# A linear-attention and token-mixing kernel on one core: V's parts issued apart, the output weights in three transfers, and a newly searched order of all work

## The chip, the core and the metric

The kernel runs on one NeuronCore of a Trainium2 chip. Five engines work side by side, each through its own list of instructions in order: TensorE (PE; its weight loads are shown as PEld), VectorE (DVE), ScalarE (ACT), GpSimd (POOL) and SyncE (SP), which here only issues transfers. Transfers between the chip's main memory and the on-chip memory are carried out by 16 DMA engines. Matmul results go to PSUM, eight banks of on-chip accumulators, from which VectorE and ScalarE copy them out. The metric is the device time of one launch in microseconds; the profile shows one execution.

## What is computed

Two layers follow each other. The first is a recurrence with decay over 768 time steps, for 4 batches and 8 heads of width 48; the second mixes tokens:

```python
# first layer: y, for every batch and head
cur = u*k_t (outer) v_t
y_t = r_t @ (state + cur)
state = w_t[:, None] * state + k_t (outer) v_t

# second layer on x = y with the heads side by side (4, 768, 384)
wq, wk = x @ w_q, x @ w_k                      # d_hyper = 64
mixed  = (wq @ wk.T) / sqrt(64) @ x            # per batch, 768 x 768 weights
out    = relu(mixed) @ w_out                   # 384 x 384
```

Inputs and output are float32, 4.7 MB for each of r, k, v, w and for the output, 0.8 MB for the weights.

## The kernel before

The time steps are cut into 12 units (n = 0 to 11) of 256 steps, three to a batch; a unit holds two chunks of 128 steps. Each unit needs four tiles of 128 rows x 768 floats (384 KB): `wg`, `kg`, `rg` and `vg`, each from a ring of four buffers, so that the tile of unit n + 4 can be loaded once the tile of unit n has been read. The work of a unit, by the names that stand in the profile:

- `lw` = ln of w (L536, ScalarE); a matmul with the mask `CM` gives its sums along time, and two exponentials of them, `ep` and `en` (L589, L595, ScalarE).
- casts of k, r and v to bf16: `k16`, `r16` (L547; shown as k and r) and `v16` (L687; shown as v), on GpSimd, ScalarE or, for unit 0, VectorE. k and r are transposed on TensorE; `ks` is the copy of k transposed, `qT` = r times ks, `RT` = r times ep (L650), `KT` = k times en (L663, on GpSimd or VectorE; L658 for the first and last unit).
- `VB` is v with its rows sorted (a matmul and a copy); `dd` the diagonal with u, `Vd` = VB times dd (L725).
- `AM` = masked scores of a chunk (L746, VectorE); `kd` (L454 to L462) the keys for the state; `SB` the state (L809); `X` = the first layer's output (L851, VectorE).
- per unit of the second layer: `XT` (X transposed and copied), the products with w_q and w_k, copied to `QK`; per batch `T` and its copy `TS`; per unit again `mx` and its relu `MX` (L466 on ScalarE, L468 on VectorE), the product with w_out, its copy `os`, and the store (L977).

Helpers record most operations, so many groups share a line: L306 is every matmul, L454 and L460 are the plain copies of ScalarE and VectorE.

Nothing is scheduled while the kernel is built. Every operation is a step of the class `Plan`, with an engine or a choice of engines, a duration, and the steps that it waits for. Two tables that were searched beforehand settle the rest: `RANK` gives each step's place on its engine, `ALT` the engine or form for each step that has a choice. `Plan.order` walks through the steps with these tables and a model of durations and of transfers, gives out the PSUM banks and buffers on the way, and emits the instructions in the order in which it placed them. The durations of the model have no effect on the chip but through that order.

Transfers are steps of SyncE. The tile of v of the units 2 to 11 (`SPARE`) is loaded in three transfers that one step issues one right after the other: 64 rows, 63 rows and 1 row (`cuts`). The three weight matrices are one step of three transfers, the output weights (576 KB) in one of them; their three casts (L494 to L496) are one step of GpSimd. Outputs are stored by SyncE, but for the last one, which ScalarE issues. In the model of `order` there is a queue `Q` and a queue `R` of transfers: each transfer takes `dur` on Q and `high` on R, instruction fetches block R for a while, and a transfer starts only when the third one before it has moved.

TensorE also runs 39 matmuls of zeros (`Z`) at the start and in gaps of the first units.

Of the kernel before, what the change touches and what calls it, by code (L numbers as in the profile page):

```python
# [33 lines left out]
class Plan:  # L34
# [8 lines left out]
    ASIDE, BLOCKED = 1200, 1000  # L43
# [45 lines left out]
    def dma(self, key, issue, dur, fn, after=(), buf=None, reads=(), behind=None, high=None):  # L89

        i = self.add(key, {"S": issue}, fn, after, buf, lag=0, behind=behind)
        m = self.add(key + ("wire",), {"Q": (dur, dur if high is None else high, None)}, None, [i], lag=0)
        l = self.add(key + ("land",), {"L": self.LAND}, None, [m], lag=0, reads=reads)
        return i, l

    def order(self):
# [5 lines left out]
        wires = {}  # L102
# [6 lines left out]
        owners, moved, done, mode = [None] * 8, [], [], 0  # L109
# [14 lines left out]
        def start(s):  # L124
# [7 lines left out]
            if s["eng"] == "S" and len(moved) >= 3:  # L132
                t = max(t, moved[-3])
# [30 lines left out]
        while True:  # L164
# [14 lines left out]
            if e == "E":  # L179
                mode = s["mode"]  # L180
            took = s["dur"] + self.SWITCH * change
            n = s["opts"][s["way"]][5]
            if n:
                first = count
                count += n
                while count > edge:
# [5 lines left out]
                    free["R"] = max(free["R"], cross + self.ASIDE) + self.BLOCKED  # L192
                    edge += self.BLOCK
            lock = s["lock"] and e == "D"
            if lock:
                took += max(0, free["P"] - t)
            run(s, t, took)
            if lock:
                free["P"] = max(free["P"], t + took)
            if s["i"] in wires:  # L200
                m = wires[s["i"]]
                free["Q"] = max(free["Q"], s["end"]) + m["dur"]
                free["R"] = max(free["R"], s["end"]) + m["mode"]
                m["start"], m["end"] = s["end"], max(free["Q"], free["R"])
                done.append(m)
                moved.append(m["end"])
# [849 lines left out]
```

## Time and profile before

| | us |
|---|---|
| median of 3 runs | 106.12 |
| range of these | 105.59 to 106.23 |
| profiled execution | 106.6 |
| its span, first to last instruction | 104.8 |
| mean granted TensorE clock | 0.984 of full |

Busy shares overlap, since the engines work side by side. A row of the view by stretch gives for each engine its busy time in that stretch and, in brackets, its instructions; then the granted TensorE clock, the mean share in which the DMA engines were occupied (above 1 where packets overlap) and the rate. A row of a group gives busy time and mean duration (ns) of one instruction, then the idle time of the engine just before it and what ended that. A row of the chain or of the timeline gives start, duration and work. SPq, ACTq and so on are the engines' issuing sides: the duration of an issue includes the time in which it is held up.

### The profile page before, as it was taken

Reading aid. Unit: us, or ns where it says so; the run is one execution under the profiler, and the core shown is the slowest. Engines: PE = TensorE matmul, PEld = TensorE weight load, DVE = VectorE, ACT = ScalarE, POOL = GpSimd, SP = SyncE. Lnnn points to the kernel's source line nnn. Section 1 sums busy time; section 2 is a strip of 40 time slices with the busy share of each in tenths; the row PEclk is TensorE's granted clock in tenths of the full one; section 3 lists DMA queues with packets and bytes.
Section 4 is the critical chain, followed back from the end, with each engine's and each line's share of the span. In section 5 each row is a group of like instructions: output and inputs, shape, how many; then the busy total and the mean of one; then the engine's idle time right before and its main releaser. Section 6 shows DMA issues by size and latency. Waiting matters only on the chain.

```text
span 104.8 us, 5072 instructions
## 1 busy us (share of the span) xinstructions
PE 91.6 (87%) x2201; PEld 65.7 (63%) x2201; DVE 84.3 (80%) x152; ACT 80.0 (76%) x117; POOL 66.9 (64%) x70
## 2 busy tenths in 40 slices
PE   6999998887699789999589689998999999999940
PEld 2264885485567558786375577865777778787510
DVE  5539999898699939999789699998999899857630
ACT  4359879989777298795996988999959898873830
POOL 4433695978998936988589779779995910400000
PEclk9999999999999957999999999999999999999999
DMA  1999997989999999889898999999989100029784
GB/s 33 317 323 325 325 318 183 282 228 244 264 315 267 235 298 248 215 199 280 226 228 199 248 304 307 222 317 301 304 283 326 43 0 6 6 111 367 274 287 172
DMA packets 53488, 24.71 MB, mean 236 GB/s; under 512 B 51162, under 2 KB 52314, under 8 KB 53466
## 3 DMA queue, kind: packets, MB, share of 16 engines
q1 hardware_dynamic: 53306, 24.19, 83.4%
q8 instruction: 17, 0.28, 1.1%
q10 hardware_dynamic: 160, 0.20, 0.5%
q14 instruction: 5, 0.04, 0.1%
HBM read 19.66 MB, written 4.72 MB: 233 GB/s over the span
## 4 chain that ended last, share of the span: by engine, by line
PE 38%; DMA 26%; SPq 9%; ACT 8%; POOL 6%; issue 5%; DVE 4%; POOLq 0%; ACTq 0%; DVEq 0%
PE PS L306 38%; DMA wg<-in_w_dram 13%; DMA vg<-in_v_dram 8%; SPq L364 8%; DMA kg<-in_k_dram 5%; ACT MX L466 3%; DVE AM L746 2%; POOL r L547 2%; POOL k L547 2%; POOL Vd L725 1%; ACT os L454 1%; ACT en L595 1%; SPq L977 1%; DVE VB L460 1%; ACT lw L536 1%
## 5 line engine op out<-in xcount | busy, mean ns | idle before, releaser
L746 DVE TENSOR_TENSOR AM<-PS,US 128x1024 bf16<-128x1024 f32 x24 | 29.0, 1220 | 2.8 <-PE PS L306 2.8
L725 POOL TENSOR_TENSOR Vd<-VB,dd 128x768 bf16<-128x768 bf16 (+1 forms) x13 | 17.6, 1353 | 8.3 <-DVE dd L460 6.1
L663 POOL TENSOR_TENSOR KT<-ks,en 128x1024 bf16<-128x1024 bf16 x10 | 21.3, 2129 | 0.8 <-ACT ep L589 0.7
L595 ACT ACTIVATE en<-PS,dn 128x1024 bf16<-128x1024 f32 (+1 forms) x14 | 13.9, 992 | 2.9 <-PE PS L306 2.4
L306 PE MATMUL PS<-Z 128*128 128x512 bf16 (+1 forms) x43 | 14.8, 432 | 1.1 <-DVE Z L380 1.0
L536 ACT ACTIVATE lw<-wg 128x768 bf16<-128x768 f32 x12 | 10.1, 842 | 6.3 <-DMA wg<-in_w_dram 6.2
L589 ACT ACTIVATE ep<-PS,up 128x1024 bf16<-128x1024 f32 (+1 forms) x14 | 13.9, 1011 | 1.0 <-PE PS L306 0.8
L306 PE MATMUL PS<-wo,MX 128*128 128x384 bf16 (+1 forms) x93 | 13.8, 327 | 0.3 <-ACT MX L466 0.3
L306 PEld LDWEIGHTS <-KT 48*128 48x128 bf16 x352 | 9.1, 95 | 6.9 <-issue 4.0
L547 POOL CAST k<-kg 128x768 bf16<-128x768 f32 x10 | 8.3, 825 | 6.0 <-DMA kg<-in_k_dram 4.7
L851 DVE TENSOR_TENSOR X<-PS,Vd 128x768 bf16<-128x768 f32 (+1 forms) x13 | 11.5, 892 | 0.7 <-PE PS L306 0.4
L306 PE MATMUL PS<-RT,KT 48*128 48x128 bf16 x192 | 9.9, 220 | 1.4 <-ACT QK L454 0.9
L466 ACT ACTIVATE MX<-PS 128x768 bf16<-128x768 f32 (+1 forms) x14 | 9.4, 700 | 1.9 <-PE PS L306 1.9
L687 POOL CAST v<-vg 128x768 bf16<-128x768 f32 x9 | 7.4, 827 | 4.3 <-DMA vg<-in_v_dram 4.1
L547 POOL CAST r<-rg 128x768 bf16<-128x768 f32 x10 | 8.3, 827 | 2.3 <-DMA rg<-in_r_dram 2.3
L650 DVE TENSOR_TENSOR RT<-PS,ep 128x1024 bf16<-128x1024 bf16 (+1 forms) x14 | 8.4, 607 | 1.6 <-PE PS L306 1.4
L454 ACT CAST VB<-PS 128x768 bf16<-128x768 f32 x11 | 8.9, 807 | 1.0 <-issue 0.6
L454 ACT COPY os<-PS 128x768 f32<-128x768 f32 (+1 forms) x10 | 7.0, 702 | 3.3 <-PE PS L306 2.1
L306 PEld LDWEIGHTS <-MX 128*128 128x128 bf16 (+1 forms) x93 | 7.1, 103 | 3.5 <-ACT MX L466 0.4
L306 PE MATMUL PS<-CM,lw 64*128 64x128 bf16 x192 | 8.2, 231 | 1.2 <-ACT lw L536 1.0
L641 DVE TENSOR_TENSOR qT<-PS,ks 128x1024 bf16<-128x1024 bf16 x12 | 8.2, 683 | 0.4 <-PE PS L306 0.3
L809 DVE TENSOR_TENSOR SB<-PS,ep 128x192 bf16<-128x192 f32 x20 | 7.0, 350 | 1.8 <-PE PS L306 1.7
(88 smaller groups left out, 184.9 us busy)
## 6 DMA issues: line engine op xcount, KB each, us to landing
wg<-in_w_dram SPq DMA_DIRECT2D x12, 384.0 KB
kg<-in_k_dram SPq DMA_DIRECT2D x12, 384.0 KB
rg<-in_r_dram SPq DMA_DIRECT2D x12, 384.0 KB
out_dram<-os SPq DMA_DIRECT2D x9, 384.0 KB
vg<-in_v_dram SPq DMA_DIRECT2D x10, 192.0 KB
vg<-in_v_dram SPq DMA_DIRECT2D x10, 189.0 KB
out_dram<-os SPq DMA_DIRECT2D x5, 192.0 KB
vg<-in_v_dram SPq DMA_DIRECT2D x2, 384.0 KB
```

The lines of the kernel that those rows point to most:

```text
L306: return nc.tensor.matmul(o, l, rr, start=start, stop=stop, skip_group_check=True, is_transpose=trans)
L454: nc.scalar.copy(o, i)
L466: nc.scalar.activation(o, i, ACT.Relu)
L536: nc.scalar.activation(view(lw.tile, 0, [[64, H], [512, 2], [1, D]]), view(g["wg"].tile, 0, [[D2, H], [D, 2], [1, D]]), ACT.Ln, bias=0.0, ...
L547: op(view(o.tile, 0, [[64, H], [512, 2], [1, D]]), view(g[src].tile, 0, [[D2, H], [D, 2], [1, D]]))
L589: nc.scalar.activation(view(ep.tile, cs[0] * NP * EW + RS, [[EW, n4], [1 - RS, 2], [1, R]]), view(at(cw), cs[0] * 512, [[C, n4], [R, 2], [ ...
L595: nc.scalar.activation(en.tile[:, ds(cs[0] * 512, w_)], at(cw)[:, ds(cs[0] * 512, w_)], ACT.Exp, bias=dn, scale=-1.0)
L650: nc.vector.tensor_tensor(view(RT.tile, cs[0] * 512, [[512, len(cs)], [R, H], [1, R]]), view(at(kr, BF16), cs[0] * apart + second, [[apart ...
L663: x.tensor_tensor(KT.tile[:, w], ks.tile[:, w], en.tile[:, w], ALU.mult)
L725: (nc.vector if e == "D" else nc.gpsimd).tensor_tensor(Vd.tile[:, cols], VB.tile[:, cols], view(dd.tile, cs[0] * H, [[1, len(cs) * H], [0, ...
L746: AMs[c] = add(("AM", n, c), {"D": 1221}, lambda e, c=c, A=A: nc.vector.tensor_tensor(view(AM[c].tile, 0, [[C, 8], [1, C]]), view(at(A), 0 ...
L851: lambda e, c0=c0, nc_=nc_: nc.vector.tensor_tensor(view(X.tile, (2 * i + c0) * DM, [[D2, NP * nc_], [D, 2], [1, D]]), view(at(y), c0 * NP ...
```

## The change

Every operation stays. Five things change.

1. The model of transfers inside `Plan.order`: no wait for the third transfer before, no fetch blocks on R; instead an issue ends once the work still queued on Q and on R has fallen below a limit each (`DEEP`), and a tile takes 1500 on R (1220 in the first two units). This code is for the search; on the chip it acts through the order alone.
2. V of the units 2 to 11 is three steps instead of one, so that other transfers may stand between its parts: 63 rows, 1 row, 64 rows. The cast `v16` waits for all three.
3. The weights are two steps: w_q and w_k, and the output weights in three transfers of 63, 63 and 2 rows. The casts wait for both.
4. `RANK` and `ALT` are new throughout: the order on all engines and the choice of engines and forms.
5. The class's durations for some DMA steps.

```diff
-    ASIDE, BLOCKED = 1200, 1000
+    DEEP = dict(Q=1850, R=2500)
...
-            if s["eng"] == "S" and len(moved) >= 3:
-                t = max(t, moved[-3])
...
-                    free["R"] = max(free["R"], cross + self.ASIDE) + self.BLOCKED
...
+            if s["i"] in wires:
+                m = wires[s["i"]]
+                x = t + took
+                full = [0]
+                for q, d in (("Q", m["dur"]), ("R", m["mode"])):
+                    if d:
+                        free[q] = max(free[q], x)
+                        full.append(free[q] + m["opts"]["Q"][5] * d // max(m["dur"], 1) - self.DEEP[q])
+                        free[q] += d
+                m["start"] = x
...
+                took = max(took, max(full) - t)
...
-            nc.sync.dma_start(out=view(wo_f, 0, [[DM, NK], [1, DM]]),
-                              in_=moe_w_out.rearrange("(n p) d -> p n d", p=128))
-        l = plan.dma(("wts",), 1800, 2700, f)[1]
+
+        def f_o(e):
+            for p, z in ((0, 63), (63, 126), (126, 128)):
+                nc.sync.dma_start(out=view(wo_f, 0, [[DM, NK], [1, DM]], p0=p, pn=z - p),
+                                  in_=moe_w_out.rearrange("(n p) d -> p n d", p=128)[ds(p, z - p)])
+        l = [plan.dma(("wts",), 1000, 700, f, deep=900, high=850)[1],
+             plan.dma(("wtso",), 1500, 3300, f_o, high=0, deep=800)[1]]
...
-        wts["qk"] = wts["o"] = add(("wcast",), {"P": 2650}, cast, [l])
+        wts["qk"] = wts["o"] = add(("wcast",), {"P": 2650}, cast, l)
...
-            cuts = (0, 64, 127, C) if name == "vg" and n in SPARE else (0, C)
-            g[name + "L"] = plan.dma((name, n), 570 * (len(cuts) - 1) if "S" in begun else 1055,
...
+            t, issue, rest = 1220 if n < 2 else 1500, 500 if "S" in begun else 1055, None
+            if name == "vg" and n in SPARE:
+                g["vl"] = [plan.dma(("vl", n), 500, 1065, lambda e, f=f: f(e, p0=64, p1=127),
+                                    buf=g[name], high=0)[1]]
+                g["vl"].append(plan.dma(("vk", n), 500, 20, lambda e, f=f: f(e, p0=127, p1=C),
+                                        buf=g[name], high=0)[1])
+                g["vgL"] = plan.dma((name, n), 500, 610, lambda e, f=f: f(e, p0=0, p1=64),
+                                    buf=g[name], high=750)
+            else:
+                g[name + "L"] = plan.dma((name, n), issue, 1220, f, buf=g[name], high=t,
+                                         behind=begun.get("S") if n == 0 else None)
...
-                view(g["vg"].tile, 0, [[D2, H], [D, 2], [1, D]])), [g["vgL"]], v16, [g["vg"]])
+                view(g["vg"].tile, 0, [[D2, H], [D, 2], [1, D]])), [g["vgL"]] + g.get("vl", []), v16,
+                [g["vg"]])
```

In the built program this gives the following order of transfers around the middle and the end of the loads (unit in brackets, rows of a part behind the colon):

```
before: ... w8 v8:64 v8:63 v8:1 r8 k8 w9 r9 k9 w10 v9:64 v9:63 v9:1 w11 k10 r10 r11 k11 v10:64 v10:63 v10:1
        store store v11:64 v11:63 v11:1 store ...
after:  ... k8 k9 w8 v8:63 w9 r8 v8:1 v8:64 store v9:63 v9:1 r9 r10 w10 k10 v9:64 store v10:63 w11 v11:63 v11:1
        r11 v10:1 v10:64 k11 v11:64 store ...
```

The engines' work by count: two KT, one wide Vd and two r casts leave GpSimd; VectorE has two KT, one wide Vd, two wide MX and one ks more and three XT, one VB, one wide os and one r less; ScalarE has three r, three XT, one VB and one wide os more and two wide MX, one ks, one wide kd and one v less. TensorE issues 2,220 matmuls instead of 2,201, since some steps use the form with 64 columns of weights at a time where others give it up.

More of the change, by code (lines that the diff above doesn't have):

```diff
@@ L87, in add, with dma @@
         return s
-    def dma(self, key, issue, dur, fn, after=(), buf=None, reads=(), behind=None, high=None):
+    def dma(self, key, issue, dur, fn, after=(), buf=None, reads=(), behind=None, high=None,
+            deep=None):
         i = self.add(key, {"S": issue}, fn, after, buf, lag=0, behind=behind)
         m = self.add(key + ("wire",), {"Q": (dur, dur if high is None else high, None)}, None, [i], lag=0)
+        m["opts"]["Q"][5] = dur if deep is None else deep
         l = self.add(key + ("land",), {"L": self.LAND}, None, [m], lag=0, reads=reads)
@@ L108, in order @@
         rings = {k: [] for k in self.rings}
-        owners, moved, done, mode = [None] * 8, [], [], 0
+        owners, done, mode = [None] * 8, [], 0
         count, edge, ready = 0, self.FIRST, 0
@@ L196, in order @@
                 took += max(0, free["P"] - t)
+            if s["i"] in wires:
[8 more added lines that the diff above has]
+                m["start"] = x
+                m["end"] = max([x] + [free[q] for q, d in (("Q", m["dur"]), ("R", m["mode"])) if d])
+                took = max(took, max(full) - t)
+                for q, d in (("Q", m["dur"]), ("R", m["mode"])):
+                    if d:
+                        free[q] = max(free[q], t + took)
+                        m["end"] = max(m["end"], t + took)
             run(s, t, took)
@@ L360, with load @@
     dn = const([C, 1], F32, "dn")
-    def load(b, i, tl, ap, cuts=(0, C)):
-        for p, z in zip(cuts, cuts[1:]):
-            nc.sync.dma_start(
-                out=view(tl, 0, [[D2, H], [1, D2]], p0=p, pn=z - p),
-                in_=ap[b, :, ds(i * U + 2 * p, 2 * (z - p))].rearrange("h (p j) d -> p h (j d)", j=2))
+    def load(b, i, tl, ap, p, z):
+        nc.sync.dma_start(
+            out=view(tl, 0, [[D2, H], [1, D2]], p0=p, pn=z - p),
+            in_=ap[b, :, ds(i * U + 2 * p, 2 * (z - p))].rearrange("h (p j) d -> p h (j d)", j=2))
     def load_whole(b, q, tl):
```

22 lines of the change are left out of this document (8 added, 14 removed), and 70 rows, old and new, of the table RANK.

## The prediction, made before the result was known

> **What bounds the kernel now.** I read the page first (busy shares, transfer rate, chain of waits), then busy time by stretch, then the chain in order of time, and last the groups of instructions by shape.
>
> ```profile
> PE 91.6 (87%) x2201; PEld 65.7 (63%) x2201; DVE 84.3 (80%) x152; ACT 80.0 (76%) x117; POOL 66.9 (64%) x70
> ...
> PE 38%; DMA 26%; SPq 9%; ACT 8%; POOL 6%; issue 5%; DVE 4%; POOLq 0%; ACTq 0%; DVEq 0%
> ```
>
> No engine is full, and a quarter of the chain is waiting for transfers. The next view cuts the span at the places where the feeding changes, and at 83.58 us, where VectorE starts the first product of the last unit. Columns: PE, PEld, DVE, ACT, POOL busy, granted clock, share of the DMA engines, GB/s.
>
> ```profile
> 5.40:16.00 10.60, 10.57 (x183) 7.18 (x182) 8.65 (x17) 8.16 (x13) 6.45 (x8) 1.00 1.15 318
> 17.00:18.00 1.00, 0.98 (x26) 0.66 (x25) 1.00 (x3) 1.00 (x3) 0.30 (x1) 1.00 0.70 191
> 16.00:36.00 20.00, 17.29 (x476) 12.69 (x475) 17.41 (x27) 15.77 (x21) 17.20 (x16) 1.00 0.97 252
> 36.00:42.00 6.00, 5.03 (x103) 3.56 (x101) 4.28 (x8) 5.31 (x8) 3.56 (x4) 0.72 1.05 276
> 42.00:50.00 8.00, 7.52 (x233) 5.97 (x230) 7.64 (x12) 6.09 (x11) 7.35 (x7) 1.00 0.93 234
> 50.00:60.00 10.00, 7.46 (x200) 5.39 (x196) 8.01 (x12) 9.05 (x13) 7.85 (x7) 1.00 0.89 222
> 60.00:70.00 10.00, 9.71 (x279) 7.61 (x279) 9.63 (x16) 8.87 (x13) 7.82 (x8) 1.00 1.13 286
> 70.00:83.58 13.58, 12.91 (x359) 9.61 (x353) 12.41 (x20) 11.45 (x17) 12.27 (x11) 1.00 0.83 259
> 16.00:83.58 67.58, 59.92 (x1628) 44.83 (x1627) 59.38 (x89) 56.54 (x80) 56.05 (x49) 0.97 0.96 254
> 83.58:104.80 21.22, 16.70 (x386) 12.39 (x382) 13.58 (x27) 13.16 (x24) 1.78 (x2) 1.00 0.41 151
> ```
>
> Up to 16 us the loads run at 318 GB/s. After that the same queue gives 254 on average: 254 x 67.58 is 17.2 MB, which at 318 would take 54 us, so the stream has about 13 us of slack that it spends idle or uneven. At 17 to 18 us, with V in its three parts under way, the rate is 191 at a share of 0.70: 0.6 of 318 and 1.15.
>
> VectorE is the fullest engine of the middle: 59.38 of 67.58 us, 0.879. The shortfall sits in three stretches, 16 to 36, 36 to 42 and 50 to 60: 29.70 of 36 us (0.825). The other three hold 29.68 of 31.58, 0.940, and the best single one 0.963. The chain says what starves the bad ones and what the end hangs on.
>
> ```profile
> 27.62 8.40 DMA wg<-in_w_dram
> ...
> 36.10 0.85 ACT lw L536
> ...
> 76.68 4.35 DMA vg<-in_v_dram
> ...
> 81.95 0.84 POOL k L547
> 82.79 0.05 issue
> 82.83 3.39 PE PS L306 x94
> ```
>
> The w of unit 5 lands 8.40 us after its issue; ScalarE, VectorE and TensorE run dry, and the granted clock falls to 0.72 just there. At the end the last V lands at 81.03, its cast goes first, and the k of the last unit is cast only at 81.95 although it was loaded before: everything of unit 11 starts from that cast.
>
> **The change part by part.** The operations are the same; what moves is the order on every engine, who does which copy, and the order of the transfers.
>
> *Who does what.* By count of the two orders against these groups:
>
> ```profile
> L650 DVE TENSOR_TENSOR RT<-PS,ep 128x1024 bf16<-128x1024 bf16 x10 | 6.8, 684 | 1.6 <-PE PS L306 1.4 <-issue 0.3
> L851 DVE TENSOR_TENSOR X<-PS,Vd 128x768 bf16<-128x768 f32 x11 | 10.5, 953 | 0.4 <-PE PS L306 0.2
> L460 DVE COPY ks<-PS 128x1024 bf16<-128x1024 bf16 x10 | 6.9, 687 | 1.6 <-PE PS L306 1.4
> L460 DVE COPY XT<-PS 128x768 bf16<-128x768 bf16 x6 | 3.3, 551 | 0.1
> L460 DVE COPY os<-PS 128x768 f32<-128x768 f32 x2 | 1.9, 959 | 0.5 <-PE PS L306 0.5
> L462 DVE TENSOR_SCALAR kd<-PS 128x768 bf16<-128x768 bf16 x2 | 1.1, 558 | 0.3 <-PE PS L306 0.3
> L547 DVE CAST r<-rg 128x768 bf16<-128x768 f32 x1 | 0.6, 560 | 0.8 <-DMA rg<-in_r_dram 0.8
> L725 DVE TENSOR_TENSOR Vd<-VB,dd 128x384 bf16<-128x384 bf16 x1 | 0.6, 559 | 0.0
> L468 DVE TENSOR_SCALAR MX<-PS 128x384 bf16<-128x384 f32 x1 | 0.6, 558 | 1.0 <-PE PS L306 1.0
> ...
> L466 ACT ACTIVATE MX<-PS 128x768 bf16<-128x768 f32 x9 | 7.2, 817 | 0.9 <-PE PS L306 0.9
> L454 ACT COPY XT<-PS 128x768 bf16<-128x768 bf16 x5 | 4.0, 794 | 0.2 <-PE PS L306 0.2
> L547 ACT CAST r<-rg 128x768 bf16<-128x768 f32 x1 | 0.8, 846 | 0.0
> L454 ACT COPY ks<-PS 128x1024 bf16<-128x1024 bf16 x2 | 2.0, 1012 | 1.1 <-PE PS L306 1.1
> ...
> L663 POOL TENSOR_TENSOR KT<-ks,en 128x1024 bf16<-128x1024 bf16 x10 | 21.3, 2129 | 0.8 <-ACT ep L589 0.7
> L725 POOL TENSOR_TENSOR Vd<-VB,dd 128x768 bf16<-128x768 bf16 x10 | 14.8, 1478 | 1.6 <-DVE VB L460 1.6
> L547 POOL CAST r<-rg 128x768 bf16<-128x768 f32 x10 | 8.3, 827 | 2.3 <-DMA rg<-in_r_dram 2.3
> ```
>
> VectorE gives up three XT (3 x 0.551), a VB and a wide os (0.959 each; the VB has the os's shape) and an r (0.560): 4.13 us. It takes two KT, one wide Vd, two wide MX, a ks (0.687), a wide kd (0.558) and a narrow os (0.558, by the narrow MX). No row shows a wide KT, Vd or MX on VectorE. KT lies between the 0.684 of RT, a product of the same size, and GpSimd's 2.129; I take 0.684, RT being the same engine. Vd lies between its narrow 0.559 and GpSimd's 1.478; I take X's 0.953. MX I take as the wide os, 0.959. Together 6.04, so VectorE gains 1.9 us of work (with the upper ends 5.3). The narrow copies left over on both sides I let cancel. ScalarE takes three r, three XT, a VB and an os and gives two MX, a ks, a v and a wide kd (taken as an r and an XT): 3 x 0.846 + 5 x 0.794 - 2 x 0.817 - 1.012 - 0.846 - 0.794, 2.2 us more; it gives back five narrow copies for two, so 2.2 is an upper end, and it idles 11 us in the middle (56.54 of 67.58), which covers it. GpSimd sheds two KT, a Vd, two r and takes a v: 4.26 + 1.48 + 0.83, 6.6 us less.
>
> *The last unit.* In the new order an X (0.953) no longer stands on VectorE between the last unit's first products and its masks, where the old one has it, and on TensorE 359 matmuls instead of 418 stand from the last k transposes on. Fifty-nine at 16.70/386 = 43 ns are 2.5 us. So the tail shortens by between 0.95 and 2.5; I take 0.95, since X lies on a chain of products and the matmuls also fill gaps. What leaves the tail has to be done before: VectorE's middle is then 59.38 + 1.9 + 0.95 = 62.2 us of work. On GpSimd the last k is now cast before the last v, so that the v landing no longer holds it; but the last k load itself is now the last but one transfer.
>
> *V in parts.* The 64-row, the 63-row and the 1-row part are now separate steps, placed apart with whole tiles between them. Same bytes, same number of issues. The 0.6 ratio at 17 us is what parts side by side cost; between whole tiles that loss can be covered by them. The price: V is complete only with its last part, one to five transfers later than before from unit 3 on, and a v cast that waits holds GpSimd's queue: behind the casts of units 5 and 6 stand KT of 6 and k of 7. A whole tile is 393 kB, 1.24 us at 318; so 1.2 to 6.2 us if the stream keeps its present pace, nothing if it gains as much of its 13; I take nothing, and the slower case below holds the other end.
>
> *The weights.* One 590 kB transfer becomes 63 + 63 + 2 rows: 1.85 us at 318, 3.1 at 191. The casts of the weights now stand on GpSimd ahead of v of unit 3 and k and r of unit 4. Between 0 and 1.2 us; GpSimd's 2.8 idle us from 16 to 36 hide it and I take 0. Two more issues of SyncE take the 0.49 of the row below each; SyncE's issue of a tile lasts 1.22 us where 0.49 can do, so they pass in its waits.
>
> *Stores and early loads.*
>
> ```profile
> 25.51 0.49 SPq L489 DMA_DIRECT2D wof<-in_moe_w_out_dram  x1
> ...
> 57.67 0.78 ACT L454 COPY os<-PS 128x768 f32<-128x768 f32 x1
> 59.61 1.22 SPq L364 DMA_DIRECT2D kg<-in_k_dram  x1
> ...
> 12.77 0.82 POOL L547 CAST k<-kg 128x768 bf16<-128x768 f32 x1 [0.20 <-DMA kg<-in_k_dram]
> 19.26 2.13 POOL L663 TENSOR_TENSOR KT<-ks,en 128x1024 bf16<-128x1024 bf16 x1
> ```
>
> The first store now has 38 tiles ahead of it and ten behind it, and waits for ScalarE's first os. In the old order SyncE has issued 38 tiles by 59.61 and that copy ends at 58.45; so the store stops no load unless the stream is over 1 us ahead, and even then seven tiles and two stores at 1.24 and three V's at 1.6 (half at 318, half at 191), 16 us in all, bring the last landing to between 75 and, with the 4.35 us that the old last V took from issue to landing, 79 us, against 81.03. Early on, k of unit 2 goes from the 8th to the 12th place among the tiles: it lands four tiles and 0.4 us for the uneven V later, at 18.1 instead of 12.7; r lands a tile after it at 19.4, its cast takes 0.83, and KT, which stands behind that cast, begins at 20.2 instead of 19.26: 0 to 1.0 us, and I take 0.8, nearer the upper end, since KT's place leaves no choice.
>
> *The sum.* With VectorE's middle at the 0.940 that the undisturbed stretches show, 62.2 us of work take 66.2: -1.4. Tail -0.95, unit 2 +0.8. That is -1.5 on a span of 104.8; the profiled execution took 106.6, 1.8 above its span, and the median of the runs is 106.12, so 104.6.
>
> **The rivals.**
>
> *VectorE becomes the bound and the end is later.* The 1.9 us come from an engine with slack (56.05 of 67.58) to the fullest one. If loads still come as late as now, 0.879, then 62.2 takes 70.8, +3.2, less 0.95: 108.4. It decides at 62.2/68.5 = 0.908: below that the kernel is slower. For it: the V's complete later, the late unit 2. Against it: 60 to 70 us ran at 0.963 with the loads at 286 GB/s.
>
> *The stream runs tight.* All at 0.963: 62.2 takes 64.6, -2.9, with the tail 102.3. For it: 13 us of slack in the stream; against it, 70 to 83.58 us is well supplied and still at 0.914.
>
> *The parts move nothing.* The waits change place only and half of the shortfall stays, 0.91: 68.4, +0.8, less 0.95: 106.0. The Trainium skill, DMA: Bandwidth & Descriptors, Rules for kernel authors, says not to cut a transfer in partition halves, since both halves use the same engines one after the other; by that rule the parts gain nothing wherever they stand. The trace agrees only in part: at a share of 0.70 against 1.15 the engines are not all in use.
>
> *VectorE's products wait for GpSimd.* Two KT, a wide and a narrow Vd read two tensors of on-chip memory beside a busy GpSimd. A GpSimd operation lasts 56.05/49 = 1.14 us there; half of it at a share of 0.83 is 0.47, four times 1.9 us, which would make 106.5. The Trainium skill, SBUF — State Buffer, on the shared port pair, says that such a VectorE operation and a GpSimd one that reads that memory exclude each other for a whole instruction. No row of this profile shows the pair.
>
> **How the numbers follow.** The forecast, 104.6 (own range 103.6 to 105.6), gets 0.38; the slower VectorE 0.26; the tight stream 0.14; parts that move nothing 0.11; the products' waits 0.11. About 1% (105.06 and 107.18) is what a measurement of this kernel can tell from no change. Faster: 0.30 of the forecast, the tight stream and a little of the next, 0.45. Slower: 0.24 of the second case and 0.06 of the last two, 0.30. Same: 0.25. The range, 102.5 to 108.3, leaves out half of the tight stream and under half of the slower case.
>
> **What would show it.** In the profile after: VectorE busy 86 us, GpSimd 60; the middle's VectorE share near 0.94 with no clock below 1.00 around 36 us; a rate over 280 GB/s from 16 us on; the cast of the last k ending before 82 us; fewer than 20 us from the last unit's first KT to the end. The forecast is wrong if the middle's share stays under 0.908, if SyncE stands at its first store while loads wait behind it, or if KT on VectorE takes well over 0.684.

## The result and the profile after

| | before | after |
|---|---|---|
| median, us (four runs each, side by side) | 106.18 | 111.97 |
| range, us | 105.59 to 108.35 | 110.92 to 113.66 |
| profiled execution, its span | 106.6, 104.8 | 112.78, 111.1 |

The changed kernel is slower: ratio 1.047, 95% interval 1.041 to 1.053. Runs of one version spread by up to 4 us here, some of them disturbed; ratios use the undisturbed ones alone, and where too few were left for a ratio the median of all runs of that version stands.

First the page of the kernel after: busy shares, then the granted clock and the rate in 40 slices of 2.78 us, then the chain of waits.

```profile
PE 96.7 (87%) x2220; PEld 68.0 (61%) x2220; DVE 85.6 (77%) x156; ACT 81.7 (74%) x117; POOL 60.2 (54%) x66
...
PEclk9999999999995589999556999999999999999999
...
GB/s 46 321 317 317 319 261 259 249 227 174 143 246 260 211 247 272 209 188 191 249 276 312 250 302 245 288 260 257 222 227 108 6 0 6 227 297 200 191 350 167
...
PE 42%; SPq 16%; DVE 15%; DMA 9%; ACT 7%; issue 4%; POOL 3%; POOLq 0%; DVEq 0%; ACTq 0%
```

VectorE and GpSimd do the work that was counted out (85.6 and 60.2 us). But the rate falls to 143 in the eleventh slice (27.8 to 30.6 us), the clock falls to about half two slices later, and the pair comes again: 188 GB/s at 47 to 50 us, the clock at half from 53. SyncE's issuing side, 9% of the chain before, is now 16%.

The same kernel by stretch; columns as in the prediction. The first row is the middle up to VectorE's first product of the last unit, the second the tail.

```profile
16.00:91.39 75.39, 66.63 (x1704) 50.16 (x1705) 62.40 (x95) 60.83 (x85) 51.91 (x45) 0.91 0.91 219
91.39:111.10 19.71, 15.70 (x321) 10.34 (x317) 12.18 (x24) 11.20 (x21) 1.62 (x2) 1.00 0.54 202
...
22.00:32.00 10.00, 7.10 (x191) 5.34 (x193) 8.16 (x12) 5.53 (x9) 6.43 (x6) 1.00 0.79 182
32.00:40.00 8.00, 7.29 (x148) 5.14 (x142) 4.56 (x8) 5.32 (x7) 4.24 (x5) 0.57 1.04 248
42.00:50.00 8.00, 7.22 (x185) 5.30 (x187) 8.00 (x13) 6.24 (x9) 4.56 (x4) 1.00 1.01 219
53.00:60.00 7.00, 6.45 (x144) 5.06 (x145) 4.42 (x6) 5.31 (x9) 6.90 (x7) 0.52 1.11 279
```

The span grew by 6.3 us: the middle from 67.58 to 75.39 us, +7.81, the tail from 21.22 to 19.71, -1.51. VectorE's work in the middle, 62.40 us, is what the prediction had (62.2); its share is 62.40/75.39 = 0.828 instead of 0.940.

Where the first dry spell comes from shows in the timeline of SyncE's issues: start, duration, line, transfer, count.

```profile
20.61 1.51 SPq L503 DMA_DIRECT2D wof<-in_moe_w_out_dram  x3
22.24 0.39 SPq L375 DMA_DIRECT2D wg<-in_w_dram  x1
22.68 7.21 SPq L375 DMA_DIRECT2D vg<-in_v_dram  x3
29.99 0.56 SPq L375 DMA_DIRECT2D kg<-in_k_dram  x1
```

and in the timelines of the engines that wait for it:

```profile
30.88 0.84 ACT L558 ACTIVATE lw<-wg 128x768 bf16<-128x768 f32 x1 [2.69 <-DMA wg<-in_w_dram]
...
31.78 0.62 PE L318 MATMUL PS<-CM,lw 64*128 64x128 bf16 x16 [2.38 <-ACT lw L558]
...
34.11 0.83 POOL L709 CAST v<-vg 128x768 bf16<-128x768 f32 x1 [2.82 <-DMA vg<-in_v_dram]
```

Behind the three transfers of the output weights the three parts of V of unit 3 hold SyncE for 7.21 us. The w of unit 4 is issued at 22.24, just before them, and its logarithm starts at 30.88; ScalarE has waited 2.69 us for it, TensorE waits 2.38 for the logarithm, GpSimd 2.82 for the V. The engines that move data are in use for only 0.79 of 22 to 32 us, at 182 GB/s.

### The profile page after: what moved, and what is told of

It reads as the page before. It is cut to its first block, busy times and chain, and to the rows that moved or that the text cites. A ratio compares the mean times of both kernels' runs of the same rounds, so it can differ in the third digit from the quotient of the medians.

```text
span 111.1 us, 5110 instructions
## 1 busy us (share of the span) xinstructions
PE 96.7 (87%) x2220; PEld 68.0 (61%) x2220; DVE 85.6 (77%) x156; ACT 81.7 (74%) x117; POOL 60.2 (54%) x66
## 4 chain that ended last, share of the span: by engine, by line
PE 42%; SPq 16%; DVE 15%; DMA 9%; ACT 7%; issue 4%; POOL 3%; POOLq 0%; DVEq 0%; ACTq 0%
PE PS L318 42%; SPq L375 16%; DMA vg<-in_v_dram 9%; DVE AM L769 7%; ACT en L617 3%; POOL KT L685 2%; ACT ep L611 2%; DVE qT L663 2%; POOL v L709 2%; DVE RT L672 1%; DVE X L874 1%; DVE ks L471 1%; DVE SB L832 1%; ACT lw L558 1%; ACT XT L465 1%
## 5 line engine op out<-in xcount | busy, mean ns | idle before, releaser
L685 POOL TENSOR_TENSOR KT<-ks,en 128x1024 bf16<-128x1024 bf16 x8 | 17.1, 2132 | 6.7 <-DVE ks L471 3.0
L748 POOL TENSOR_TENSOR Vd<-VB,dd 128x768 bf16<-128x768 bf16 (+1 forms) x12 | 15.7, 1318 | 8.9 <-DVE dd L471 6.3
L318 PE MATMUL PS<-Z 128*128 128x512 bf16 (+1 forms) x43 | 16.0, 441 | 1.3 <-DVE Z L391 1.0
L709 POOL CAST v<-vg 128x768 bf16<-128x768 f32 x10 | 8.2, 828 | 9.5 <-DMA vg<-in_v_dram 8.7
L318 PEld LDWEIGHTS <-KT 48*128 48x128 bf16 (+1 forms) x368 | 9.9, 102 | 5.1 <-issue 2.4
L318 PE MATMUL PS<-RT,KT 48*128 48x128 bf16 (+1 forms) x200 | 10.2, 236 | 0.5 <-DVE AM L769 0.2
L318 PE MATMUL PS<-CM,lw 64*128 64x128 bf16 (+1 forms) x208 | 7.6, 219 | 3.4 <-ACT lw L558 2.4
L477 ACT ACTIVATE MX<-PS 128x768 bf16<-128x768 f32 (+1 forms) x12 | 8.0, 682 | 1.7 <-PE PS L318 1.1
L318 PEld LDWEIGHTS <-lw 64*128 64x128 bf16 (+1 forms) x208 | 6.0, 98 | 4.8 <-ACT lw L558 2.7
L569 POOL CAST r<-rg 128x768 bf16<-128x768 f32 x8 | 6.6, 830 | 3.9 <-DMA rg<-in_r_dram 2.0
```

Of the source, the lines that this page charges most:

```text
L318: return nc.tensor.matmul(o, l, rr, start=start, stop=stop, skip_group_check=True, is_transpose=trans)
L569: op(view(o.tile, 0, [[64, H], [512, 2], [1, D]]), view(g[src].tile, 0, [[D2, H], [D, 2], [1, D]]))
L685: x.tensor_tensor(KT.tile[:, w], ks.tile[:, w], en.tile[:, w], ALU.mult)
L748: (nc.vector if e == "D" else nc.gpsimd).tensor_tensor(Vd.tile[:, cols], VB.tile[:, cols], view(dd.tile, cs[0] * H, [[1, len(cs) * H], [0, ...
```

## The experiments

**Which of the cuts.** Four kernels: the changed one with one cut or both undone, and the old one with the weights' cut alone.

```diff
# e1 (after), e3 (after)
-            for p, z in ((0, 63), (63, 126), (126, 128)):
+            for p, z in ((0, 128),):
# e2 (after), e3 (after)
-                g["vl"] = [plan.dma(("vl", n), 500, 1065, lambda e, f=f: f(e, p0=64, p1=127),
+                g["vl"] = [plan.dma(("vl", n), 500, 1065, lambda e, f=f: f(e),
...
-                g["vl"].append(plan.dma(("vk", n), 500, 20, lambda e, f=f: f(e, p0=127, p1=C),
+                g["vl"].append(plan.dma(("vk", n), 500, 20, lambda e: None,
...
-                g["vgL"] = plan.dma((name, n), 500, 610, lambda e, f=f: f(e, p0=0, p1=64),
+                g["vgL"] = plan.dma((name, n), 500, 610, lambda e: None,
# e4 (before)
-            nc.sync.dma_start(out=view(wo_f, 0, [[DM, NK], [1, DM]]),
+            for p, z in ((0, 63), (63, 126), (126, 128)):
+                nc.sync.dma_start(out=view(wo_f, 0, [[DM, NK], [1, DM]], p0=p, pn=z - p),
```

> The new order with the output weights in one transfer of 128 rows instead of 63, 63 and 2; nothing else. Theory W (the two 63-row transfers of the weights, with a 63-row part of V close behind them, load a part of the DMA engines alone; SyncE stands from 22.68 to 29.99 us, the w of unit 4 comes late and TensorE runs dry and then slow): the stand of 7.2 us shrinks to under 4, the share of TensorE's full clock in 32 to 40 us is above 0.9, and 3 to 4 of the 4.8 us over the kernel before come back: 107 to 108.5. Theory V (the parts of V set apart do it, the second dry spell at 50 to 53 us is theirs, and the first too): under 1 us comes back, 110 to 111. Theory O (the order and the work moved to VectorE are to blame, whatever the transfers look like): 110 to 111.5, and the clock falls somewhere else.

> The new order with each V of units 2 to 11 in one transfer of 128 rows at the place of its 63-row part; the weights stay in 63, 63 and 2. Theory V: the second dry spell goes (SyncE's 7.0 us at 44.96 to 52.0 shrink to under 5), 2 us or more come back, 107 to 109. Theory W: the first dry spell stays, though one 63-row transfer less lies behind the weights; 109 to 110.5. Theory O: 110 to 111.5.

> The new order with both the weights and every V in one transfer of 128 rows. If the transfers' shape is all of it (W and V together), the time falls to that of the kernel before or under it: 104.5 to 106.5. If W alone counts, as the first experiment gives, within 1 us of it. If the order alone counts (O): 110 to 111.5. A result between, 107 to 109, leaves that much to the order.

> The kernel before, with its order, but the output weights in transfers of 63, 63 and 2 rows at the place of the one. Theory W: the transfers behind them (k and r of unit 4, w of unit 5) come 1 to 3 us later than now, and w of unit 5 is already what TensorE waits for at 36 us: 107.5 to 109. Theories V and O: within 0.7 us of the kernel before, 105.5 to 106.9.

Measured: weights whole 110.05; V whole 107.55 (ratio to before 1.014, 1.007 to 1.021); both whole 107.22; the old kernel with the weights cut 110.34 (1.038, 1.028 to 1.047). The kernel before ran at 106.72 beside them. No theory has all four times: weights whole lies where V and O had it, V whole where V had it, the old kernel with the cut even above what W had, and both whole at 107 to 109, the result that leaves a part to the order. One row by stretch of each, first of the old kernel as it was:

```profile
22.00:32.00 10.00, 8.28 (x230) 6.25 (x223) 8.28 (x12) 8.59 (x11) 8.74 (x9) 1.00 0.98 269
```

With the weights whole:

```profile
22.00:32.00 10.00, 9.46 (x237) 6.66 (x230) 9.64 (x16) 7.99 (x12) 7.86 (x8) 1.00 1.09 291
```

With V whole:

```profile
22.00:32.00 10.00, 7.34 (x197) 5.39 (x193) 7.85 (x13) 6.07 (x10) 7.27 (x7) 1.00 0.92 213
```

With both whole:

```profile
22.00:32.00 10.00, 9.16 (x236) 6.69 (x236) 9.27 (x14) 8.22 (x11) 8.17 (x9) 1.00 1.05 299
```

The old kernel with the weights cut:

```profile
22.00:32.00 10.00, 8.20 (x248) 6.41 (x243) 8.11 (x12) 8.23 (x10) 8.08 (x8) 1.00 0.94 208
```

In the last column the rate is 291 and 299 with the weights whole, 213 and 208 with them cut, in either order: the dry stretch of 22 to 32 us belongs to the weights. (In the old order VectorE is as busy there with the cut as without, 8.11 and 8.28 us; the loss comes later.) The second fall of the rate belongs to V's parts: from 42 to 50 us the changed kernel has 219 GB/s, and with the weights alone whole it stays low,

```profile
42.00:50.00 8.00, 5.29 (x168) 4.14 (x164) 6.14 (x12) 6.33 (x8) 3.97 (x4) 1.00 1.04 204
```

while with both whole the rate is back:

```profile
42.00:50.00 8.00, 5.99 (x176) 4.54 (x174) 6.71 (x13) 6.54 (x9) 4.91 (x4) 1.00 1.04 272
```

The weights' cut costs 111.97 - 110.05 = 1.9 us in the new order and 110.34 - 106.72 = 3.6 in the old one. V's cut costs 110.05 - 107.22 = 2.8 in the new order, with the weights whole. The two overlap: taken the other way round, V's cut costs 111.97 - 107.55 = 4.4 and the weights' cut only 107.55 - 107.22 = 0.3. And these are differences of medians of runs that spread by up to 3 us: by the fastest run of each kernel (110.92, 108.18, 107.30, 105.09) they are 2.7 and 3.1, or 3.6 and 2.2. So in the new order the weights' cut costs between 0.3 and 2.7 us and V's between 2.8 and 4.4, and these times fix neither more closely.

**What in a cut costs.** My first theory was that a transfer of 63 rows occupies only part of the engines that move data, so that cuts at 64 rows should be free. Four kernels: the weights as 64 + 64 rows in the old order; V in one piece, and as 64 + 64, in the old order; everything as 64 + 64 in the new one.

```diff
# e5 (before), e8 (after)
+            for p, z in ((0, 64), (64, 128)):
# e6 (before)
-                                     lambda e, ap=ap, x=g[name].tile, cuts=cuts: load(b, i, x, ap, cuts),
+                                     lambda e, ap=ap, x=g[name].tile: load(b, i, x, ap),
# e7 (before)
+                     load(b, i, x, ap, (0, 64, C) if len(cuts) > 2 else cuts),
# e8 (after), beside the 1-row part left out
-                g["vl"] = [plan.dma(("vl", n), 500, 1065, lambda e, f=f: f(e, p0=64, p1=127),
+                g["vl"] = [plan.dma(("vl", n), 500, 1065, lambda e, f=f: f(e, p0=64, p1=C),
```

> The kernel before, with the output weights in two transfers of 64 rows each instead of one of 128; nothing else. The same cut in 63, 63 and 2 rows gave 110.3 (1.038 of before), with 208 GB/s between 22 and 32 us. Theory of the rows (a transfer of 63 rows occupies only part of the DMA engines and holds up SyncE's next issues): 64 rows occupy them all, so 106 to 107, the rate from 22 to 32 us back over 245 GB/s, no issue of SyncE of over 3 us there. Theory of the number (any further transfer in the queue costs): two transfers instead of one are half of the extra of three, so about 108.3, and a rate near 230. Theory of the descriptors (the bytes come in smaller pieces): the pieces are the same in all cuts, so it gives 106 to 107 here and cannot explain 110.3.

> The kernel before, with V of units 2 to 11 in one transfer of 128 rows instead of 64 + 63 + 1 issued one right after the other; order and all else the same. Theory of the rows: the old cut costs the old kernel too, so 103.5 to 106, rate from 16 to 83 us over the 254 GB/s of before. Rival (the cut with its parts side by side is what the old order was searched for, since a part that lies on few DMA engines leaves the rest to the next tile): 107 to 109. Theory that the parts move nothing when they stand together: within 0.5 us of before.

> The kernel before, with V of units 2 to 11 in two transfers of 64 rows, issued one right after the other, instead of 64 + 63 + 1. Theory of the rows: like V whole, within 0.7 us of that run. Theory of the number: between V whole and before. If V whole should be slower than before, this one tells whether it was the number of transfers (then it stays at before) or the 63 rows (then it goes with V whole).

> The kernel after, with the output weights in 64 + 64 rows and V in 64 + 64 rows, the second 64 at the place of the 63-row part and the 1-row part gone; the parts of V still stand apart and V is still complete only with the last of them. Theory of the rows: about what both whole gave, 107.2 (106.2 to 108.2), no stretch of 2 us in which TensorE stands, no clock below 0.8 after it. Theory of the number and of V complete late: 109 to 112, the stand of SyncE at V of unit 3 still over 5 us.

Measured: 108.26 (1.021, 1.008 to 1.033), 103.77 (0.970, 0.947 to 0.993), 106.37 (1.004, 0.998 to 1.010) and 111.45 (1.050, 1.034 to 1.065). The theory fell: V as 64 + 64 rows costs the old kernel what 64 + 63 + 1 cost it, and the changed kernel stays at 111.45. For the weights 64 + 64 rows cost about half of what 63 + 63 + 2 did, 1.021 against 1.038, just as the theory of the number had it. V whole makes the old kernel faster than both kernels of this case, so the old cut was a cost there too. That left two theories, the number of transfers and the rows that they cover. Loads alone decide between them.

```python
# e9: eight tiles in each stretch
for ap, first, f in ((r, 0, whole), (k, 0, halves), (v, 0, three), (w, 0, columns),
                     (r, 4, lower), (k, 4, middle), (v, 4, odd), (w, 4, whole)):
    for i in range(8):
        f(first + i, T[i], ap)
    seen_all()
```

> Loads alone: no step of the computation, outputs are stored as zeros. Eight tiles of 393 kB per stretch, from the tensors of this case, each stretch issued by SyncE and ended before the next one begins: whole tiles; 64 + 64 rows; 64 + 63 + 1 rows; two halves of the columns with all 128 rows; rows 0 to 63 alone; rows 32 to 95 alone; rows 64 to 126 alone; whole again. Theory of the half of the rows (a transfer that writes only rows 0 to 63 or 64 to 127 goes at about half of the rate, however its engines are occupied): whole 300 to 325 GB/s, column halves the same, rows 0 to 63 alone 160 to 200, 64 + 64 side by side between the two, rows 32 to 95, which lie in both halves, near the whole rate. Theory of the number (each transfer costs a fixed time): column halves as slow as 64 + 64, rows 0 to 63 and 32 to 95 alike. Theory of the rows that do not divide: 64 + 64 like whole, only the parts with 63 rows under 250.

One row by stretch for each form, in that order. In the run SyncE issues the first transfers of a stretch while the last of the one before still land, so each row takes a time that lies inside its stretch. Columns here: stretch, length, VectorE and GpSimd busy, clock, share in which the engines that move data were occupied, GB/s.

```profile
6.00:12.00 6.00, 2.43 (x8) 0.00 (x0) 1.00 1.17 325
16.00:26.00 10.00, 0.92 (x6) 0.00 (x0) 1.00 1.29 232
30.00:40.00 10.00, 0.92 (x6) 0.00 (x0) 1.00 0.77 198
46.00:52.00 6.00, 0.77 (x5) 0.00 (x0) 1.00 1.08 292
55.50:61.00 5.50, 0.77 (x5) 0.00 (x0) 1.00 1.32 193
64.00:67.00 3.00, 0.86 (x6) 0.00 (x0) 1.00 1.12 300
69.50:75.50 6.00, 0.92 (x6) 0.00 (x0) 1.00 0.67 179
81.00:86.00 5.00, 0.62 (x4) 0.00 (x0) 1.00 1.16 320
```

Whole tiles go at 325 GB/s with the engines at a share of 1.17, rows 0 to 63 at 193 with a share of 1.32: the engines are occupied and slow. Rows 32 to 95, as many rows and as many bytes, go at 300, and halves of the columns at 292, a tenth below whole. So it is not the number of transfers: a transfer that stays within rows 0 to 63 goes at about 0.6 of the rate. Rows 64 to 127 alone were not run, but rows 64 to 126 go at 179, and two halves of 64 rows side by side make 232, not 325. The part of 63 rows has a second fault: its share is 0.67, half of the 1.32, so about half of the engines stand idle; in rate that costs little more, 179 against 193. With the 1-row part a V in three pieces goes at 198, 0.61 of whole. The Trainium skill, SBUF — State Buffer, on the DMA port swizzle, has the rule: the rows decide how many of the 16 ports a transfer reaches, rows 0 to 63 reach half of them, and 196 GB/s stand there against 328 for 128 rows; 193 against 325 here agrees. For the 63 rows, the Trainium skill, DMA: Bandwidth & Descriptors, on why a DMA increments its semaphore by 16, says that the number of engines is the largest one up to 16 that divides the rows, 9 for 63; 0.67/1.32 = 0.51 against 9/16 = 0.56.

Then the same in the kernels: the pieces as columns of all 128 rows, with as many transfers, and V as late as before.

```diff
# e10 (after), beside the 1-row part left out
+                g["vl"] = [plan.dma(("vl", n), 500, 1065, lambda e, f=f: f(e, h0=H // 2, h1=H),
...
+                g["vgL"] = plan.dma((name, n), 500, 610, lambda e, f=f: f(e, h0=0, h1=H // 2),
...
-            for p, z in ((0, 63), (63, 126), (126, 128)):
+            for n in range(NK):
+                nc.sync.dma_start(out=wo_f[:, ds(n * DM, DM)], in_=moe_w_out[ds(n * 128, 128)])
# e11 (before), in load()
-        for p, z in zip(cuts, cuts[1:]):
+        for h, g in ((0, H // 2), (H // 2, H)) if len(cuts) > 2 else ((0, H),):
```

> The kernel after, with every part as a piece of the columns of all 128 rows: V as two halves of its heads at the places of the 63-row and the 64-row part, no 1-row part; the output weights in three transfers of 128 rows x 384. As many transfers as with 64 + 64 rows, which gave 111.4, and V is complete as late. Theory of the half of the rows: 106 to 108.5, as with all whole (107.2), no stand of SyncE over 4 us, no clock under 0.8. Theory of the number, or of V complete late: 110 to 112.5.

> The kernel before, with V of units 2 to 11 in two transfers of half of the heads each, all 128 rows, issued one right after the other. Theory of the half of the rows: as with V whole, 103 to 104.8. Theory of the number: as with 64 + 64 rows, 105.7 to 107.

Measured: 106.58 (0.998, 0.991 to 1.005) and 104.20. Both as the theory of the half of the rows has it, and SyncE stands nowhere over 3.2 us while it issues loads; the number of transfers and the late V cost nothing that these times show. With the pieces turned from rows to columns the changed kernel loses all that it was slower.

**The clock.** In the profile after, 15 us go at a clock of 0.52 to 0.57. Matmuls of zeros in front of the three steps for which TensorE stood keep it up.

```diff
+        def keep(o, times, cols=512):
+            for _ in range(0 if tally else times):
+                nc.tensor.matmul(o[:, ds(512 - cols, cols)], Z, view(Z, 0, [[0, cols // C], [1, C]]),
...
+            keep(x, 10 if n == 4 else 0)
+                keep(at(kr), 8 if n == 6 and name == "rT" else 0, 256)
+                keep(at(vp), 4 if n == 6 else 0)
```

> The kernel after with 22 matmuls of zeros more, placed ahead of the three steps for which TensorE stood: ten of 128x512 ahead of the sums of unit 4 (it stood from about 29.4 to 31.7 us), eight of 128x256 ahead of the transposes of the r of unit 6 (50.4 to 51.4) and four of 128x512 ahead of the product with the v of unit 6 (52.6 to 53.5). They write banks that the following step overwrites; no result changes, and the transfers stay as they are. Theory that the fall of the clock is a cost of its own: no clock below 0.9 at 32 to 40 and at 53 to 60 us, and 107.5 to 109.5, since 14 us at about 0.55 would go at full clock. Theory that the late transfers alone set the end, and the clock only stretches work that would wait: the clock stays up and the time stays within 1 us of 111.5.

Measured: 112.03 (1.051, 1.039 to 1.062). The same stretches as above, by that profile:

```profile
22.00:32.00 10.00, 9.51 (x204) 6.35 (x202) 8.01 (x12) 5.97 (x9) 5.83 (x6) 1.00 0.94 237
32.00:40.00 8.00, 7.49 (x193) 5.49 (x190) 7.33 (x12) 5.85 (x9) 6.30 (x5) 1.00 1.03 254
40.00:50.00 10.00, 8.69 (x190) 6.57 (x189) 8.45 (x12) 6.76 (x9) 4.54 (x4) 0.83 1.01 204
50.00:60.00 10.00, 8.79 (x216) 6.15 (x217) 7.65 (x12) 8.79 (x12) 8.30 (x8) 1.00 1.06 265
```

The clock holds at 32 to 40 and at 50 to 60 us and falls once, at 40 to 50. The mean clock of the four runs was 0.984 to 1.00, against 0.937 to 0.963 after, and the time is the same. That looks like the second theory, but the zeros have a price of their own. In the same profile, the logarithm of unit 4, the zeros and the sums that wait for both:

```profile
28.57 0.85 ACT L558 ACTIVATE lw<-wg 128x768 bf16<-128x768 f32 x1 [1.02 <-DMA wg<-in_w_dram]
...
28.70 2.33 PE L595 MATMUL PS<-Z 128*128 128x512 bf16 x10
30.96 0.62 PE L318 MATMUL PS<-CM,lw 64*128 64x128 bf16 x16
```

The logarithm ends at 29.42, earlier than the 31.72 of the changed kernel, but the zeros run on to 31.03 and the sums start only at 30.96, 1.5 us late. The last four zeros, 1.02 us, stand before the second of two products with v (53.56 us), whose cast had ended at 52.63, while the wait is for the first (0.62 us). So the experiment doesn't decide what the low clock costs: up to 2.5 us that the zeros take away could hide as much gain. It shows that the clock can be held up there and that the kernel gains nothing by these zeros.

**What is left: the order itself.** With all transfers whole the new order takes 107.2 and the old one 103.8, by the two kernels above (by the fastest run of each, 105.09 and 102.04). Three kernels ask whether SyncE's order or VectorE's added work makes these 3.4 us.

```diff
# e13 (e3) and e14 (e6): SyncE's steps in the other kernel's order
+        for x, name in enumerate(LOADS.split()):
+            own[name]["rank"] = x
# e15 (e3): three steps back on GpSimd
+        x = {("KT", 1, 0): 8.5, ("KT", 3, 0): 14.5, ("Vd", 4, 0): 23.5}.get(s["key"])
```

> The kernel after with V and the output weights whole (107.2), and SyncE's loads in the order of the kernel before; the order and the choice of every other engine stay those of after. The kernel before with V whole gave 103.8: 3.4 us between the two stay unexplained by the cuts. Theory of the loads' order (k of units 8 and 9 ahead of w of unit 8, VectorE 10.5 of 14 us busy from 46 to 60): 103.5 to 105, VectorE over 12.3 of 14 from 46 to 60. Theory of VectorE's work (62.4 to 63.5 us in the middle instead of 58.9 to 59.4, at the same share of 0.89): 106.5 to 108, the share of the middle still about 0.89.

> The mirror: the kernel before with V whole (103.8), its transfers in the order of the kernel after; the two first stores stay ahead of the last load, all other engines as before. Theory of the loads' order: 106.5 to 108, a dry stretch of VectorE between 46 and 60 us. Theory of VectorE's work: 103 to 104.8.

> The kernel after with V and the output weights whole (107.2), with the KT of units 1 and 3 and the wide Vd of unit 4 on GpSimd again, at the places that they have there in the kernel before; all else as after. VectorE loses 2 x 0.68 + 0.95 = 2.3 us of work. Theory of VectorE's work: 2.3 / 0.89 = 2.6 us less, 104.2 to 105.2. Theory of the loads' order: within 0.8 us of 107.2, since VectorE waits for loads anyway. Rival of both (KT at 2.13 us on GpSimd comes too late for its unit): over 108.

Measured: 111.64 (1.048, 1.039 to 1.058), 107.57 (1.010, 0.997 to 1.024) and 109.82 (107.04 to 110.29). Each exchange of loads makes its kernel slower by some 4 us. The first lies outside both theories; the second has the time of the loads' order, but not at the place that was expected. By stretch, first the new order with the old loads:

```profile
16.00:22.00 6.00, 4.04 (x78) 3.06 (x77) 3.33 (x7) 2.58 (x4) 4.15 (x5) 0.72 1.04 274
...
46.00:60.00 14.00, 10.02 (x273) 7.26 (x269) 10.40 (x15) 12.81 (x18) 9.17 (x9) 1.00 1.02 269
```

Then the old order with the new loads:

```profile
16.00:22.00 6.00, 2.07 (x42) 1.23 (x38) 1.68 (x3) 1.42 (x3) 3.33 (x3) 0.75 1.01 268
...
46.00:60.00 14.00, 13.13 (x381) 10.02 (x378) 13.60 (x21) 13.96 (x21) 12.76 (x12) 1.00 0.98 258
```

The stretch of 46 to 60 us stays poor (VectorE 10.40 of 14) with the old loads and is full (13.60) with the new ones, so its fill goes with the engines' order and not with that of the loads. What both exchanges starve is 16 to 22 us: VectorE is busy for 3.33 and 1.68 of 6 and the clock falls, though the loads come at 274 and 268 GB/s. (In the second kernel GpSimd's cast of a k waits 5.5 us there for its load, in the first TensorE waits for a cast of v.) Loads and engines are ordered for each other.

The third kernel doesn't gain 2.6 us: its median lies 2.6 above that of the same kernel without the change, its fastest run 2.0 above (107.04 against 105.09). That is the rival in which KT on GpSimd comes too late (over 108), and its profile shows a second price:

```profile
15.02 2.12 POOL L685 TENSOR_TENSOR KT<-ks,en 128x1024 bf16<-128x1024 bf16 x1 [0.54 <-ACT en L617]
...
15.49 2.06 DVE L748 TENSOR_TENSOR Vd<-VB,dd 128x384 bf16<-128x384 bf16 x1
```

The KT of unit 1, back on GpSimd, stands in the chain of work that ended last, and the narrow Vd that VectorE starts meanwhile takes 2.06 us where it takes 0.55 in the changed kernel. So this run can't price VectorE's added work, and which places of the new order carry the 3.4 us is open.

## Why the prediction was wrong

- **The work moved and its prices: right.** The groups of the profile after, by shape:

```profile
L685 DVE TENSOR_TENSOR KT<-ks,en 128x1024 bf16<-128x1024 bf16 x2 | 1.4, 682 | 0.0
...
L748 DVE TENSOR_TENSOR Vd<-VB,dd 128x768 bf16<-128x768 bf16 x1 | 0.9, 947 | 0.0
...
L479 DVE TENSOR_SCALAR MX<-PS 128x768 bf16<-128x768 f32 x2 | 1.9, 952 | 0.0
```

  0.682, 0.947 and 0.952, where 0.684, 0.953 and 0.959 were taken.
- **The rival in which these products wait for GpSimd: not met here, but not unfounded.** In this profile GpSimd stands idle at all three places (KT at 16.41 and 33.26 us, Vd at 45.51). Where it is busy the products are longer: with V whole one KT, started just after a cast began on GpSimd, took 1.34 us, with both whole one KT took 1.17 and the Vd 1.44, and with the work given back the narrow Vd took 2.06. The prediction's 0.47 a time is near the smaller of these; what they add to the time of a kernel was not measured.
- **The tail: right in kind**, -1.51 for -0.95, inside its bounds. The last k is cast at 85.19, where the prediction wanted its cast ended before 82; the middle before it is late.
- **The first store: right.** SyncE is not held there.
- **K of unit 2 late, +0.8: late, but without a cost that shows.** Its KT begins on GpSimd at 21.94, 2.7 us later than before and 1.7 later than reckoned; still VectorE is busy for 5.50 of the 6 us from 16 on, 5.48 before. In the old engines' order the same loads do starve this place. (The sums of the rivals leave these 0.8 us out.)
- **The parts of V moved apart, "I take nothing": right with the weights whole.** There V's cut costs 2.8 us apart (new order), and 106.9 - 103.8 = 3.1 side by side (old order, by the kernel before as it ran beside that one). With the weights cut as well, as in the changed kernel, it costs 4.4. The rival in which parts gain nothing wherever they stand was right in this; against whole tiles they even cost.
- **The failed step is the middle: 62.2 us of work at a share of 0.940, which made 66.2 us.** The work was right (62.40); the share was 0.828 and the middle 75.39 us. The 0.940 came from stretches that the old order's loads fed well, and it needed a steadier supply everywhere; the rate was 219, not over 280. Three things stand behind it.
  - The reading of 191 GB/s at a share of 0.70 as engines left idle, so that "between whole tiles that loss can be covered by them". Engines do stand idle at the 63 rows, but that is the smaller fault: a transfer within rows 0 to 63 is as slow on engines that are occupied (193 GB/s at 1.32), which leaves little to cover, and set apart the parts cost about what they cost side by side. So much of the 13 us of slack in the stream was not there to be won: as an estimate from the loads alone, ten tiles of V (3.93 MB) take 12 us at 325 and 20 at 198.
  - **"GpSimd's 2.8 idle us hide it and I take 0" for the weights.** The bound on the transfer itself was fair: 590 kB last 1.8 us at 325 and 3.0 at 198, 1.2 more. But GpSimd's cast of the output weights was not what waited longest (GpSimd stands for 1.10 us before it, at 30.14); the transfers behind the weights in SyncE's queue came late, and ScalarE, TensorE and GpSimd with them. It cost 1.9 us here, if it is undone first, and 3.6 in the old order. Why it grows from 1.2 to these was not taken apart.
  - The order itself. With all loads whole the share is 0.897 in the new order (next item) and not 0.940 either.
- **The first rival, VectorE as the bound.** It said: if the share does not rise, 62.2 us of work at 0.879 make a middle of 70.8. With both cuts undone the profile has this:

```profile
16.00:86.78 70.78, 62.87 (x1705) 46.81 (x1705) 63.50 (x96) 60.41 (x85) 51.68 (x45) 1.00 0.87 235
86.78:106.50 19.72, 15.70 (x321) 10.33 (x317) 12.18 (x24) 11.19 (x21) 1.62 (x2) 0.97 0.54 203
```

  A middle of 70.78 at a share of 63.50/70.78 = 0.897. That it meets 70.8 so closely is luck in part: this execution is the slowest of its kernel (108.24; median 107.22, fastest 105.09), and the work is 63.50, not 62.2. The old kernel with V whole has nearly the same share, 58.86/65.94 = 0.893:

```profile
16.00:81.94 65.94, 58.90 (x1630) 44.00 (x1628) 58.86 (x88) 57.14 (x81) 56.13 (x49) 1.00 0.96 261
81.94:103.50 21.56, 16.70 (x386) 12.38 (x382) 13.56 (x27) 12.47 (x22) 1.78 (x2) 0.99 0.40 149
```

  So with whole transfers both orders fill VectorE alike, and the new one has more work for it in the middle. As an account of the time this rival is met, with its end below 0.908 on the slow side. As a cause it is not shown: three of the steps given back made nothing faster, in a test that brought prices of its own.

So of the 5.8 us, some 2 are the weights' cut and some 3 the order (107.22 - 103.77 = 3.4 with whole tiles, 106.58 - 104.20 = 2.4 with column pieces); V's cut costs both kernels about 3 where the weights are whole, and up to 4.4 beside the weights' cut. These shares rest on few runs and overlap. The range ended at 108.3, because its slower end held the share of the old kernel and no loss of supply on top of it.

## What to carry to other kernels

When a tile must be cut, cut its columns (292 GB/s here, against 325 whole), or take rows that lie on both sides of row 64 (300); not rows 0 to 63 and 64 to 127 (232 side by side), and not a number of rows like 63 (198 for 64 + 63 + 1). Price a cut by the whole queue behind it, not by the one engine that reads it. And before an order is searched anew, measure the forms of transfer alone: one such run here gave the rates that the argument lacked, though not what they cost in the kernel, and a piece of the old kernel that looked settled, V in three parts, turned out to be worth 3%.

## What the runs showed of the hardware

- 64 rows are not 64 rows: 193 GB/s for rows 0 to 63, 300 for rows 32 to 95, with the same bytes and the same size of piece.
- A share of the engines that move data says little of their rate: 1.32 at 193 GB/s and 1.08 at 292.
- A product on VectorE of two tensors in on-chip memory was longer where it started while a cast or a KT ran on GpSimd: KT 1.17 and 1.34 us where it takes 0.68 beside an idle GpSimd, Vd 1.44 for 0.95, a narrow Vd 2.06 for 0.55. It holds the other way too: in the changed kernel with column pieces a cast of k on GpSimd that began together with a KT on VectorE, at 31.81, took 1.37 us for 0.83.
- The granted clock fell to 0.57 and 0.52 for 8 and 7 us after dry spells in which TensorE stood for about 2.4 us, or twice for about 1. Zeros in the gaps hold it up in two of these places, but the time stayed (112.03 against 111.97); what the low clock costs by itself is open, since the zeros held up work as well.
